# The order of three groups of small products inside a step of attention on TensorE

## The chip, the cores and the metric

The kernel runs on one core of a Trainium2 chip. A time is the device time of one execution in microseconds (us), lower is better; a kernel is described by the median of several executions. TensorE appears in the profile under two names: PE for the matrix products and PEld for the loads of their stationary operands. The other engines are DVE (VectorE), ACT (ScalarE), POOL (GpSimd) and SP (SyncE, which here issues the DMAs).

## What is computed

Attention over 8 batches and 8 heads of 576 rows with 64 columns is followed by a mixture layer on all 4608 rows. The attention has two branches whose outputs are added: a pooled one, in which four neighbouring rows of q, k and v are averaged to 144 rows, and a banded one on the full 576 rows, in which a row sees only those less than 4 rows away.

```python
q_d, k_d, v_d = (t.reshape(B, H, Sd, 4, D).mean(axis=3) for t in (q, k, v))
out_up = np.repeat(sm_attn(q_d, k_d, v_d), 4, axis=2)
mask = np.abs(pos[:, None] - pos[None, :]) < 4
scores = np.where(mask, scale * np.matmul(q, k.transpose(0, 1, 3, 2)), -1e9)
out_local = np.matmul(softmax(scores), v)
x = (out_up + out_local) as [4608, 512]
h = x @ w_in;  g = h * np.clip(h + 3, 0, 6) / 6;  return g @ w_out
```

## The kernel before

A unit of attention is a pair of heads of one batch, 32 units in all. The mixture layer runs over parts of 512 rows; for each of 16 slices of the hidden width its first product (L1056, `gemm1`, 12 matmuls into a PSUM bank called h) is followed by Relu (ACT, L1062), the gate (DVE, L1066), a split into two parts, and the second product (L1106, `gemm2`, 12 matmuls into the banks called o). Two banks, h0 and h1, take turns.

A planner (`Plan.emit`) puts all work of all engines in one order with costs and due times of its own before the program is built; every engine runs its instructions in that order. For units 8 to 31 the products of attention are put on TensorE in steps, one `plan_burst` each. A step handles two units at once: it makes the scores of a new unit and, two units later, the products with v of an old one. 24 units with a lag of two give 22 steps that hold both, two at the start with scores only, and two at the end with products with v only. The planner knows a step as one operation with one cost (2.16 us for both, 1.19 us for one), whatever the order inside.

Inside a step the function `burst` calls three functions in turn. Each matmul in them is a 64x64 one, so that four of them share the array, and each is in float32, which the trace shows as two MATMUL and two LDWEIGHTS instructions.

- `scores_d4` (L537), the pooled scores: four matmuls of 144 columns into the banks a0 and a1, and four of 72 columns into spare columns of h0 and h1. It also takes the four PSUM banks for the step.
- `pv_all`: `pv` (L775), 20 matmuls of 56 to 61 columns, then `pv_d4`, four of 144 columns (L682) and four of 72 (L691). All write h0 or h1.
- `scores` (L732), the banded scores: 20 matmuls of 64 columns into a0 and a1.

After a step ACT copies the 72-column scores out of h0 and h1 (`pull`, L128), ACT and DVE combine the pooled output (`mean`, L707, and `mean_too`, L710), DVE adds the two branches (`add`, L780), which frees h0 and h1 for the first product of the mixture layer, and DVE adds the mask to the banded scores (`outside`, L748) and takes maxima (`top`, L576).

Waits between engines are semaphores. The framework gives a wait to the first instruction that needs it; a wait that the engine has already made earlier in its order is left out. A load of a stationary operand carries a wait itself; further ones stand in instructions of their own ahead of it, EVENT_SEMAPHORE, which the trace puts on TensorE's sequencer (PEldq).

Of the kernel before, what the change touches and what calls it, by code (L numbers as in the profile page):

```python
# [56 lines left out]
def tile_local_down_attention_moe(ctx, tc, q_all, k_all, v_all, _qk_loc, _v_loc, w_in, w_out, ident_d, _mask_d, out):  # L57
# [29 lines left out]
    def view(t, n, shape):  # L87
        t = t[:shape[0], :n]
        names = "abc"[:len(shape) - 1]
        return t if len(shape) == 2 else t.rearrange(  # L90
            f"p ({' '.join(names)}) -> p {' '.join(names)}", **dict(zip(names, shape[1:])))

    def buf(key, holder, shape):

        n = 1
        for k in shape[1:]:
            n *= k
        slot = plan.slot[key, holder]
        if key in late:
            return view(late[key](slot), n, shape)  # L100
        if type(slot[0]) is str:
            tag, first = PLACES[slot[0]]
            if tag not in early:
                early[tag] = wts.tile([P, 2048 if PAIRED[0] <= int(tag[1:]) < PAIRED[1] else 1024], F32, name="early", tag=tag)
            return view(early[tag][:, first + slot[1] // 4:], n, shape)
        at = slot[0]
        if at < XB:
            place = key if key == "rawd" else "xb"
            if place not in early:
                early[place] = mem.tile([P, XB // 4], F32, name="first", tag="first")  # L110
            return view(early[place][:, at // 4:], n, shape)
        if RA[0] <= at < RA[1]:
            return view(taken[:, (at - RA[0]) // 4:], n, shape)
        if at < ARENA:
            t, at = arena, at - XB - (RA[1] - RA[0] if at >= RA[1] else 0)
        else:
            t, at = rounded, at - ARENA
        return view(t[:, at // 4:], n, shape)

    def bank(key, holder):  # L120
        tag = plan.slot[key, holder]
        return psum.tile([P, 512], F32, name=tag, tag=tag)
# [194 lines left out]
    def plan_duo(b, d, masked):  # L317

        bp, b2 = divmod(b, NB2)
        row0 = (bp * P + (b2 * NHP + 2 * d) * NC) * RP  # L320
        k0 = "0" if b == 0 else ""
        PS, kv = ("s", "0") if b == 0 else ("a", "")
        due = need(b) - (1 - d) * 2 * unit_time(b)

        def early_user(o):
            if b == 0:
                early_users.append(o)
            return o

        for u in range(2):  # L330
            unit = plan_unit(b, d, u, row0, k0, kv, PS, masked, early_user, due - (1 - u) * unit_time(b) + SHIFT[NHP * b + 2 * d + u])
            if NHP * b + 2 * d + u < APART:
                for _ in unit:
                    pass
            else:
                plan_burst(unit)

    def plan_burst(unit):

        new = next(unit) if unit else None  # L340
        old = next(units[0]) if len(units) == DEPTH or units and not unit else None
        (b, u), (pb, pu) = (x and x["un"] or (None, None) for x in (new, old))
        key = (b, u) if unit else (pb, pu, "last")
        hx = [(f"h{g}x", key) for g in range(2)]

        def burst():
            hb = [bank(*h) for h in hx]
            if new:
                new["pooled"](hb)
            if old:  # L350
                old["pv"](hb)
            if new:
                new["banded"]()

        both = [x for x in (new, old) if x]
        cost = 2.16 if len(both) == 2 else 1.19
        o = op("PE", cost, burst, [a for x in both for a in x["after"]], take=hx + [t for x in both for t in x["take"]],
               free=[t for x in both for t in x["free"]], lag=LAGT, rec=52 * len(both))
        if old:
            units.pop(0).send((o, hx))  # L360
        if unit:
            unit.send((o, hx))
            units.append(unit)

    def plan_unit(b, d, u, row0, k0, kv, PS, masked, early_user, due):
# [4 lines left out]
        s_ops, sd_ops, turned, pooled = [], [], {}, {}  # L370
# [36 lines left out]
        if b < BY_PE:  # L407
            rk, evs = ("rawd", (0, d)), {}
            for i in (1, 0, 2):
# [3 lines left out]
                                  take=[key, ("qkd" + k0, un)], free=[rk], lag=LAGT, rec=1 if i == 2 else 4))  # L413
# [81 lines left out]
        if direct:  # L495
            sums = [begun["vr"], op({"POOL": on("sum4", 1.0)["POOL"]}, 0, partial(sum4, 0), [begun["v", d]],
                                    take=[("vd" + k0, un)], free=[("raw4", (0, d))])]
# [22 lines left out]
                    nc.tensor.matmul(  # L520
                        ps[hs, j * SD:(j + 1) * SD], q4[hs, j * QSTEP:j * QSTEP + QS], k4[hs], start=True, stop=True)

        def scores_d4(hb):

            for g in range(2):
                st["ps", g] = bank(PS, ("s", un, g))
            st["hb"] = hb
            stats = buf("st" + k0, ("d", un), [P, 2, 12])
            st["md"], st["sd"] = stats[:, 0, :3], stats[:, 1, :3]
            q4, k4 = qk["q", 4], qk["k", 4]  # L530
            for h, j in ((0, 0), (1, 1), (0, 2), (1, 0), (0, 1), (1, 2)):
                hs = slice(h * D, (h + 1) * D)
                a, n = QPLACE[h][j]
                for i in range(2 if n == 2 else 1):
                    ks = slice(i * SD // 2, (i + 1) * SD // 2) if n == 2 else slice(0, SD)
                    ps = rest(h, i) if n == 2 else rows_d4(n)[a * D:(a + 1) * D]
                    nc.tensor.matmul(  # L537
                        ps, q4[hs, j * QSTEP:j * QSTEP + QS], k4[hs, ks], start=True, stop=True, skip_group_check=True)

        def rest(h, i):  # L540
            return st["hb"][h][i * D:(i + 1) * D, HALF + SD:HALF + SD + SD // 2]
# [4 lines left out]
        def rows_d4(n):  # L546
            return st["pd"][:, 2] if n == 2 else st["ps", n][:, 5 * D:5 * D + SD]
# [264 lines left out]
        bk, pk, sk = (PS, ("sd", un)), ("P0" if b == 0 else "Pd", ("d", un)), ("st" + k0, ("d", un))  # L812
        bks = [(PS, ("s", un, g)) for g in range(2)]
        pl, sl = ("P0" if b == 0 else "Pl", ("l", un)), ("st" + k0, ("l", un))
        if apart:
            sd = early_user(op("PE", 0.9, scores_d, [pooled["q"], pooled["k"]], take=[bk, pk, sk], lag=LAGT, rec=12))
        else:
            sd, hx = yield {
                "un": un, "after": turned["q"] + turned["k"] + [pooled["q"], pooled["k"]] + masked,
                "take": [sk] + bks, "free": [], "pooled": scores_d4, "banded": scores}  # L820
            sl_op = sd
        sd_ops.append(sd)
        if apart:
# [14 lines left out]
        if apart:  # L838
            subs = []
            for g in range(2):  # L840
                a = op("DVE", 0.4, lambda g=g: top(rows(g), greatest(g)), [sl_op])
                subs.append(op("DVE", 0.4, lambda g=g: minus(nc.vector, st["p"][:, :, g], rows(g), greatest(g)), [a],
                               free=[bks[g]]))
# [54 lines left out]
        bks = [(PS, ("x", un, g)) for g in range(2)]  # L898
# [6 lines left out]
        else:  # L905
            a, bks = yield {
                "un": un, "after": t + lv + turned_d + sums, "take": [ok] + xbs,
                "free": [tk, vk, tk_d, ("vd" + k0, un)], "pv": pv_all}
# [853 lines left out]
class Plan:  # L1762
# [5 lines left out]
    def op(self, eng, cost, fn, after=(), take=(), free=(), size=0, dl=None, lag=0.0, lock=False, rec=0, nd=1, kind=None):  # L1768
        o = Op(len(self.ops), eng, cost, fn, take, size, dl)
        o.kind = kind  # L1770

        o.rec, o.nd = rec, nd
        o.lag, o.lock = lag, {True: ("DVE", "POOL"), False: ("POOL",)}[lock]
        self.ops.append(o)
        for a in after:
            self.dep(o, a)
        for r in free:
            self.free_after(r, [o])
        return o
# [313 lines left out]
```

## Time and profile before

| | |
|---|---|
| median of 3 executions | 896.09 us (895.85 to 897.17) |
| the profiled execution | 896.23 us, of which the span of instructions is 894.4 us |
| PE busy | 886.5 us, 99% of the span |
| DVE, ACT, POOL busy | 614.4, 430.9, 204.5 us |
| granted TensorE clock | 0.999 |

The profiled execution lies within the runs. Its span is 1.8 us shorter than its time; what lies around the span is the start and end of the launch. The page gives busy times by engine and line; the timeline gives the start of each run of like instructions; the view of a source line lists that line's instructions with the start of the first and the last.

### The profile page before, as it was taken

The page shows a single profiled execution, that of the slowest core. Times are in us where ns is not written, and L with a number is a line of the kernel's source. Part 1 is how long each engine was busy: PE and PEld are TensorE (multiplying, and loading weights), DVE is VectorE, ACT ScalarE, POOL GpSimd, SP SyncE. Part 2 cuts the span into 40 slices and gives each one's busy share as a digit, 9 for nine tenths or more (in the row PEclk, how much of TensorE's full clock was granted, in tenths as well). Part 3 has the DMA queues.
Part 4 walks back from the last instruction along what each step waited for, and adds up shares of the span by engine and source line. Part 5 has one row for each costly group of instructions (what it writes and reads, how often), then busy time and mean ns, then how long its engine had stood idle before and what let it go on. Part 6 is the DMA issues. An engine that isn't in the chain of part 4 may idle for free.

```text
span 894.4 us, 19668 instructions
## 1 busy us (share of the span) xinstructions
PE 886.5 (99%) x7068; PEld 720.9 (81%) x7068; DVE 614.4 (69%) x1164; ACT 430.9 (48%) x1442; POOL 204.5 (23%) x280
## 2 busy tenths in 40 slices
PE   9999999999999999999999999999999999999997
PEld 6677777888888888888888888888888888888886
DVE  7997876666864677657855784667566689876541
ACT  5867754644662456444642563445444155434200
POOL 5624444211512030313221130224112000000000
PEclk9999999999999999999999999999999999999999
DMA  9987543645664456724653667555642221121421
GB/s 234 300 197 250 163 130 89 126 101 102 127 151 95 87 117 140 140 56 102 138 119 77 120 128 202 119 104 114 142 105 59 55 71 48 60 82 70 149 88 48
DMA packets 316178, 107.47 MB, mean 120 GB/s; under 512 B 249520, under 2 KB 295600, under 8 KB 316080
## 3 DMA queue, kind: packets, MB, share of 16 engines
q1 hardware_dynamic: 315478, 105.44, 49.7%
q8 instruction: 56, 0.92, 0.4%
q10 hardware_dynamic: 602, 0.77, 0.3%
q14 instruction: 42, 0.34, 0.1%
HBM read 77.25 MB, written 28.90 MB: 119 GB/s over the span
## 4 chain that ended last, share of the span: by engine, by line
PE 96%; DVE 2%; ACT 1%; POOL 0%; issue 0%; DMA 0%; ACTq 0%; POOLq 0%; DVEq 0%
PE o L1106 35%; PE h L1056 34%; PE o L1321 5%; PE a L1257 5%; PE h L1257 4%; PE h L1321 2%; PE a L1321 2%; PE a L732 2%; PE h L775 2%; PE a L537 1%; PE h L682 1%; PE h L1490 1%; PE a L520 1%; PE a L703 0%; PE h L691 0%; PE h L537 0%
## 5 line engine op out<-in xcount | busy, mean ns | idle before, releaser
L1106 PE MATMUL o<-wp,rounded 128*128 128x512 f32 x1344 | 323.1, 393 | 0.0
L1056 PE MATMUL h<-rounded,wp 128*128 128x512 f32 x1332 | 313.0, 391 | 0.6 <-POOL wp L220 0.5
L1056 PEld LDWEIGHTS h<-rounded,wp 128*128 128x128 f32 x1332 | 248.8, 188 | 54.1 <-issue 1.2
L1106 PEld LDWEIGHTS o<-wp,rounded 128*128 128x128 f32 x1344 | 249.3, 188 | 53.4 <-issue 0.4
L1062 ACT ACTIVATE arena<-h 128x512 f32<-128x512 f32 x111 | 65.8, 593 | 138.6 <-PE h L1056 136.6
L1066 DVE SCALAR_TENSOR_TENSOR arena<-arena,h 128x512 f32<-128x512 f32 x111 | 75.3, 679 | 77.1 <-ACT arena L1062 76.4
L1074 DVE TENSOR_TENSOR rounded<-arena,rounded 128x512 fp32r<-128x512 f32 x75 | 52.7, 703 | 60.4 <-PE o L1106 55.0
L128 ACT CAST rounded<-arena 128x512 fp32r<-128x512 f32 (+5 forms) x87 | 53.6, 618 | 66.9 <-PE o L1106 42.9
L1074 POOL TENSOR_TENSOR rounded<-arena,rounded 128x512 fp32r<-128x512 f32 x37 | 49.3, 1333 | 144.8 <-PE o L1106 124.5
L587 ACT ACTIVATE taken<-taken,arena 128x64 f32<-128x64 f32 x240 | 80.1, 336 | 0.5
L1321 PE MATMUL o<-wp,rounded 128*128 128x512 f32 x192 | 47.8, 392 | 0.0
L130 DVE CAST rounded<-arena 128x512 fp32r<-128x512 f32 (+2 forms) x71 | 30.5, 430 | 22.5 <-PE a L1321 19.5
L587 ACT ACTIVATION_READ_ACCUMULATOR taken<-taken,arena 128x1 f32 x240 | 45.3, 189 | 0.0
L388 DVE STREAM_TRANSPOSE taken<-taken 128x576 f32<-128x576 f32 x56 | 42.7, 767 | 1.3 <-DMA taken<-in_k_dram 0.7
L466 POOL TENSOR_TENSOR arena<-arena 96x256 f32<-96x256 f32 (+1 forms) x21 | 15.4, 733 | 123.3 <-DMA arena<-in_v_dram 123.3
L1321 PEld LDWEIGHTS o<-wp,rounded 128*128 128x128 f32 x192 | 36.0, 188 | 8.0
L464 DVE TENSOR_REDUCE arena<-arena 128x128 f32<-128x512 f32 (+1 forms) x31 | 33.1, 1067 | 13.1 <-PE h L682 10.4
L604 POOL TENSOR_TENSOR taken<-taken,arena 128x432 f32<-128x432 f32 (+1 forms) x21 | 22.6, 1076 | 40.9 <-DVE arena L597 29.4
L563 ACT ACTIVATE arena<-arena 128x1 f32<-128x1 f32 (+1 forms) x78 | 15.1, 193 | 34.5 <-DVE arena L576 34.1
L467 POOL TENSOR_TENSOR arena<-arena 96x128 f32<-96x128 f32 (+1 forms) x21 | 9.5, 453 | 96.9 <-PE h L691 96.4
L128 ACT COPY taken<-h 64x72 f32<-64x72 f32 x96 | 20.3, 211 | 20.2 <-PE h L691 12.3
L420 DVE TENSOR_REDUCE arena<-taken 128x144 f32<-128x576 f32 x38 | 27.9, 747 | 1.9 <-PE h L537 0.8
(260 smaller groups left out, 1213.3 us busy)
## 6 DMA issues: line engine op xcount, KB each, us to landing
taken<-in_v_dram SPq DMA_DIRECT2D x58, 160.0 KB
rawp<-in_w_in_dram SPq DMA_DIRECT2D x16, 512.0 KB
rawp<-in_w_out_dram SPq DMA_DIRECT2D x16, 512.0 KB
taken<-in_q_dram SPq DMA_DIRECT2D x112, 72.0 KB
taken<-in_k_dram SPq DMA_DIRECT2D x112, 72.0 KB
pl<-taken SPq DMA_DIRECT2D x24, 320.0 KB
arena<-pl SPq DMA_DIRECT2D x96, 80.0 KB
arena<-in_v_dram SPq DMA_DIRECT2D x28, 256.0 KB
```

Of the source, the lines that this page charges most:

```text
L128: nc.scalar.copy(out_, in_)
L130: eng.tensor_copy(out_, in_)
L388: nc.vector.transpose(out=qk[kind], in_=qk[kind])
L464: eng.tensor_reduce(out=vd, in_=raw.rearrange("p r e -> p e r"), op=ALU.add, axis=AX.X)
L587: nc.scalar.activation(x[:, j], x[:, j], AF.Exp, bias=m[:, j:j + 1], scale=0.125, accum_out=s[:, j:j + 1])
L1056: nc.tensor.matmul(st["ps"], win[w][:, wt, kk * P:(kk + 1) * P], xs[part][:, kk], start=(kk == 0 and i == 0), stop=(kk == NK - 1 and i == ...
L1062: nc.scalar.activation(st["t"], st["ps"], AF.Relu, bias=3.0)
L1066: nc.vector.scalar_tensor_tensor(out=t, in0=t, scalar=6.0, in1=st["ps"], op0=ALU.min, op1=ALU.mult)
L1074: eng.tensor_tensor(st["gl"], st["t"], st["gh"].bitcast(F32), op=ALU.subtract)
L1106: nc.tensor.matmul(otile[n, m], gt[:, ms], wout[w][:, wt], start=(f == 0 and i == 0), stop=(f == NF - 1 and i == 2),)
L1257: nc.tensor.matmul(ps, w[:, wt, kk * P:(kk + 1) * P], x[part][:, kk], start=start and kk == 0 and i == 0, stop=stop and kk == 1 and i == 2 ...
L1321: nc.tensor.matmul(otile[n + two, m], g[:, m * P:(m + 1) * P], wout[f][:, wt], start=(f == 0 and i == 0), stop=(f == NF - 1 and i == 2), s ...
```

## The change

The order inside a step becomes: banded scores, products with v, pooled scores; and inside the pooled scores the matmuls of 72 columns come ahead of those of 144. Taking the four banks is moved out of `scores_d4` into a function `begin_scores` that runs first. A step without a new unit is as before. What the planner sees is the same: costs, dependencies and buffers of each step.

```diff
         def burst():
             hb = [bank(*h) for h in hx]
             if new:
-                new["pooled"](hb)
+                new["begin"](hb)
+                new["banded"]()
             if old:
                 old["pv"](hb)
             if new:
-                new["banded"]()
+                new["pooled"]()
...
-        def scores_d4(hb):
-
+        def begin_scores(hb):
             for g in range(2):
                 st["ps", g] = bank(PS, ("s", un, g))
             st["hb"] = hb
+
+        def scores_d4():
             stats = buf("st" + k0, ("d", un), [P, 2, 12])
...
-            for h, j in ((0, 0), (1, 1), (0, 2), (1, 0), (0, 1), (1, 2)):
+            for h, j in ((0, 1), (1, 2), (0, 0), (1, 1), (0, 2), (1, 0)):
...
-                "take": [sk] + bks, "free": [], "pooled": scores_d4, "banded": scores}
+                "take": [sk] + bks, "free": [], "begin": begin_scores, "pooled": scores_d4, "banded": scores}
```

## Rows read from the trace of the kernel before

**Rows 1.** Page: busy time of each engine; then the chain's shares by engine.
```profile
PE 886.5 (99%) x7068; PEld 720.9 (81%) x7068; DVE 614.4 (69%) x1164; ACT 430.9 (48%) x1442; POOL 204.5 (23%) x280
...
PE 96%; DVE 2%; ACT 1%; POOL 0%; issue 0%; DMA 0%; ACTq 0%; POOLq 0%; DVEq 0%
```

**Rows 2.** Windows, PE only: stretch, length, busy (instructions), clock, DMA share, GB/s.
```profile
144.00:680.00 536.00, 536.00 (x4707) 1.00 0.55 116
```

**Rows 3.** Timeline of PE, step at 220.61: start, length, line, tiles, shapes, count.
```profile
220.61 0.47 PE L537 MATMUL a<-arena 64*64 64x144 f32 x8
220.90 0.30 PE L537 MATMUL h<-arena 64*64 64x72 f32 x8
221.03 0.76 PE L775 MATMUL h<-arena,taken 64*64 64x60 f32 x40
221.60 0.43 PE L682 MATMUL h<-taken,arena 64*64 64x144 f32 x8
221.86 0.31 PE L691 MATMUL h<-taken,arena 64*64 64x72 f32 x8
221.98 0.76 PE L732 MATMUL a<-taken 64*64 64x64 f32 x40
222.67 0.50 PE L1106 MATMUL o<-wp,rounded 128*128 128x512 f32 x1
```

**Rows 4.** Lines L775, L682, L691 (172:680), L732 (span): durations ns, first, last start.
```profile
L775 PEldq EVENT_SEMAPHORE  x44: 51/51/51, 172.5 to 678.0; - x44
L682 PEldq EVENT_SEMAPHORE  x18: 51/51/51, 173.3 to 678.7; - x18
L691 PEldq EVENT_SEMAPHORE  x34: 51/51/51, 197.5 to 679.1; - x34
L732 PEldq EVENT_SEMAPHORE  x15: 51/51/51, 52.4 to 159.9; - x15
```

**Rows 5.** Timeline of PE, the step at 691.19, which has products with v only.
```profile
691.19 0.81 PE L775 MATMUL h<-arena,taken 64*64 64x60 f32 x40
691.82 0.43 PE L682 MATMUL h<-taken,arena 64*64 64x144 f32 x8
```

**Rows 6.** Timeline of PEld, the same step.
```profile
691.19 0.67 PEld L775 LDWEIGHTS h<-arena,taken 64*64 64x64 f32 x40 [0.35 <-DVE arena L597]
...
691.95 0.28 PEld L691 LDWEIGHTS h<-taken,arena 64*64 64x64 f32 x8
```

**Rows 7.** Source views: L775 in window 686.5:692.4; L691 in window 691.60:691.69.
```profile
L775 PEldq EVENT_SEMAPHORE  x4: 51/51/446, 687.0 to 688.1; - x4
...
L691 PEldq EVENT_SEMAPHORE  x1: 51/51/51, 691.7 to 691.7; - x1
```

**Rows 8.** Timeline of PE, the step at 677.87, the longest of its kind.
```profile
677.87 0.48 PE L537 MATMUL a<-arena 64*64 64x144 f32 x8
...
680.05 0.50 PE L1106 MATMUL o<-wp,rounded 128*128 128x512 f32 x1
```

**Rows 9.** Timeline of PEld, the same step, from its first load on.
```profile
677.87 0.21 PEld L537 LDWEIGHTS a<-arena 64*64 64x64 f32 x8 [0.35 <-issue]
...
679.04 0.29 PEld L691 LDWEIGHTS h<-taken,arena 64*64 64x64 f32 x6
```

**Rows 10.** Source view of L691, windows 677.80:678.97, then 679.07:679.09.
```profile
L691 PEldq EVENT_SEMAPHORE  x1: 51/51/51, 679.0 to 679.0; - x1
...
L691 PEldq EVENT_SEMAPHORE  x1: 51/51/51, 679.1 to 679.1; - x1
```

**Rows 11.** Timeline of PEld, the step at 220.61.
```profile
220.97 0.68 PEld L775 LDWEIGHTS h<-arena,taken 64*64 64x64 f32 x40
...
221.74 0.28 PEld L691 LDWEIGHTS h<-taken,arena 64*64 64x64 f32 x8
```

**Rows 12.** Timelines of ACT, DVE and PE after the step at 220.61.
```profile
222.19 0.29 ACT L707 ACTIVATE arena<-h 128x144 f32<-128x144 f32 x1 [1.09 <-PE h L691]
...
224.19 0.81 DVE L780 TENSOR_TENSOR first<-h,arena 128x288 f32<-128x288 f32 x2
...
225.53 3.33 PE L1056 MATMUL h<-rounded,wp 128*128 128x512 f32 x14
```

## Prediction

> **What bounds the kernel now.** I read the page first: PE is busy 99% of the span and makes up 96% of the chain that ended last [rows 1]. Then the windows: from 144 to 680 us, the stretch that holds all 22 steps with both units, PE is busy for all of its 536.00 us at full clock [rows 2]. So nothing else can end late there, and no wait of PE on another engine costs anything. A change in this stretch can do two things only: lengthen or shorten what PE itself does in a step, or bring a wait on another engine that isn't there now. With no idle time to win, the most that can be gained lies inside the steps.
>
> Then the timeline of one step. It takes 2.06 us from its first product at 220.61 to the next large one at 222.67 [rows 3]. The numbers to read are the distances between groups, not the lengths, since a group's length includes its last product's latency. L775 takes 221.60 - 221.03 = 0.57 us for 40 products, that is ten sets of four, 0.057 us a set. L732 takes 0.69 us with the leaving of the step, L682 0.26 us for two sets of 144 columns, L691 0.12 us for two of 72 [rows 3]. Last I read the sequencer's instructions, EVENT_SEMAPHORE, by line: this is where the order matters.
>
> **The arrangement itself costs nothing.** The same 112 products run in both orders. What could differ is the entry and the exit. Entry: the step that begins with L775 takes 691.82 - 691.19 = 0.63 us for these 40 products [rows 5] against 0.57 in the middle of a step, 0.06 more; the 144-column group takes 220.90 - 220.61 = 0.29 us at the start of a step against 0.26 for L682 in the middle [rows 3], 0.03 more. Both idle times before the first load are 0.35 us [rows 6, 9]. Exit: ten sets of L732 would be 0.57 to 0.58 in the middle of a step and take 0.69 at its end, 0.11 more; I take the same after 144 columns. Sum of the new order: 0.63 + 0.57 + 0.26 + 0.12 + 0.12 + 0.24 + 0.11 = 2.05 us against 2.06. I call it zero, with 0.03 us a step (0.7 us in all) either way.
>
> **Where the waits go.** In a step with both units L775 has two EVENT_SEMAPHOREs (44 in 22 steps), L732 none (the last one of its 15 is at 159.9, before the first of these steps) [rows 4]. In a step with products with v only, L775 has four [rows 7]. The code says why: the first product with v that writes h0, and the first that writes h1, must wait until DVE has read that bank's last contents. In a full step the pooled scores write h0 and h1 first and make these waits; in the other kind L775 makes them itself, one more per bank, and since it also waits for its v and its probabilities, each becomes one more EVENT_SEMAPHORE. In the new order the pooled scores come last, so the products with v are first on h0 and h1 in every step: I expect four EVENT_SEMAPHOREs for L775 instead of two, in two pairs, one pair ahead of the first product and one pair two products later. The banded scores, now first, get waits for their own q and k, which L775's waits covered before.
>
> **What the waits cost.** Such an instruction costs nothing as long as the sequencer is far enough ahead. How far it is ahead depends on what stands before it. Ahead of a step stand large products: the four of the step at 691.19 ran 3 to 4 us early, one of them waited 446 ns, and the idle time before the step was still 0.35 us [rows 6, 7]. So the new waits of the banded scores are free. Inside a step it is much less: the first event of L691 in that step ran at 691.68 to 691.69, while its load began at 691.95 [rows 6, 7], and at that time about two sets of L775 (to 691.82) and the two of L682 were still to start [rows 5]: three and a half to four sets. Four sets of 144 and 60 columns are 0.26 us; four sets of 64 columns, which is what will stand before L775 in the new order, are only about 0.2 us.
>
> The price of a chain of events: in the step at 677.87 two successive ones of L691 begin at 678.97 and 679.08, 0.12 us apart although each is shown with 51 ns, and the load behind the first begins at 679.04, 0.07 us after it [rows 9, 10]. So four in two pairs take 3 x 0.12 + 0.07 = 0.43 us until the load behind the last can begin, and the first pair alone 0.12 + 0.07 = 0.19. The cover is 0.20 us: the first pair fits, the load behind the second pair is 0.43 - 0.21 = 0.22 us late. Not all of it counts: at 677.87 the load behind the second event could begin at 679.08 + 0.07 = 679.15; in a regular step the loads of L691 begin 221.74 - 220.61 = 1.13 us after the start [rows 3, 11], so that this one would be due about 679.01; 0.14 late, and the step is 680.05 - 677.87 = 2.18 us [rows 8], 0.12 longer than 2.06. That also shows that a lag isn't made up: the two places of the array that fell behind kept the step longer by nearly all of it, over the ten sets of L732 that followed. So 0.22 - 0.03 = about 0.19; I take 0.18 us a step, for the first events may run a little earlier than I count. 22 steps: 22 x 0.18 = 4.0 us.
>
> Bounds: with 0.26 us of cover, as in the step at 691.19, the load is 0.16 late and the step 0.13 longer: 2.9 us. With three sets instead of four (0.17 us) it is 0.25 late and 0.22 to 0.25 longer: 5.5 us. Below nothing this term can't go, because a wait that is made later in TensorE's order saves no time where PE never waits [rows 2]. In the two steps with scores only, L732's events move to the start of the step, where they are free, and the pooled scores get none: zero.
>
> The Trainium skill, Perfetto Trace Analysis, Sequencer-only Instruction, says that the profile shows only the execution of such an instruction and neither its decode nor its wait; the trace agrees, with 0.12 us from one to the next where 51 ns are shown.
>
> **What moves for the other engines.** The products with v end about 0.2 us later by their place and 0.2 more by the delay, and the 72-column scores are last in h0 and h1, so L707 and the copies begin some 0.5 us later than now. After the step at 220.61 L707 begins at 222.19, the adds that free h0 and h1 end at 225.00, and the next product into h begins at 225.53 [rows 12], 0.53 us later, which itself moves by 0.2: hidden, and if that cover were gone it would cost the difference. The banks of the banded scores are now last written by the pooled scores, at the same time of the step as now, so L748 and L576 don't move. SP's load of the next v waits for L775 and begins 0.2 to 0.4 us later, the q and k loads up to 1.1 us earlier; both are a whole step ahead of their use. Zero.
>
> Sum: 0 + 4.0 + 0. The profiled execution has 896.23 us, 0.14 more than the median; 896.09 + 4.0 = 900.1 us.
>
> **Rivals.** (1) No cost: the sequencer is further ahead than I read, so that all four events are hidden. For it: one event of 446 ns cost nothing ahead of a step [rows 7], and most events of L691 now cost nothing; against it: the step at 677.87, where events a tenth of a microsecond late lengthened the step [rows 8 to 10]. It decides from a cover of 0.40 us, twice what I read. Time 896.1 (895.6 to 896.8). 13%.
>
> The Trainium skill, TensorE: Matmul & The Clock Gate, gives TensorE's queue 64 places; with four sets' loads and products being 32, that would be eight sets of run-ahead, 0.46 us, and rival 1. The trace reads against it, with about four sets at 691.69.
>
> (2) Part of the cost: the banded scores' waits at the start make one of the two bank waits unnecessary, three events remain, and the load is late by 0.10: 0.07 a step, 1.5 us, 897.6. 9%. (3) More cost: the sequencer, once caught up with, doesn't get ahead again within a step, and the 18 + 34 events of L682 and L691 [rows 4], hidden now, cost up to 0.12 us each, 6.2 us more: 902 to 906. For it: their cover is already thin, as 677.87 shows; against it: there L732 ran at its usual pace afterwards. 9%. (4) Faster: the excess of the few long steps (0.12 at 677.87) vanishes and no cost appears; at most 0.5 us, 895.6, since PE has no idle time to give back. Together with anything not seen, 4%. My forecast: 65%.
>
> **How the numbers follow.** This kernel's measurement tells a difference of about 0.2%, 1.8 us, from none. Slower than 897.9: the forecast, rival 3 and a little of rival 2, 0.75. Same: rival 1, most of rival 2 and the small gains of rival 4, 0.22. Faster by over 1.8 us: 0.03. The range 897.0 to 903.5 holds the forecast with its bounds (899.0 to 901.6), rival 2 and a part of rival 3; rival 1 and the far end of rival 3 are left out, 2 in 10.
>
> **What would show it.** In the profile after: L775 with four EVENT_SEMAPHOREs a step (88 in 22) would show the first step right; two or three, rivals 1 or 2. The full steps 2.2 to 2.3 us long, with gaps between L732 and L775 and two of the four places lagging, would show the second; 2.06 with four events, rival 1. PE still busy without a break and no new wait of L1056 would show the third; a wait of L1056 for L780 would make it wrong. A longer distance between L691's loads and products too would point to rival 3.

## The result and the profile after

The changed kernel takes 902.11 us (median of 4 executions, 900.74 to 902.53) beside 896.63 us for the kernel before (4 executions, 895.85 to 897.97): a ratio of 1.0055, with an interval of 1.0043 to 1.0068. It is 5.5 us slower. The profiled execution is its fastest one, 900.74 us with a span of 898.9, against a span of 894.4 before. Lines below the edit moved by two: L775, L732, L682, L691, L537 are now L777, L734, L684, L693, L539.

The page's busy times and the chain's shares by engine answer to rows 1:

```profile
PE 891.4 (99%) x7068; PEld 722.3 (80%) x7068; DVE 613.5 (68%) x1164; ACT 431.0 (48%) x1442; POOL 205.0 (23%) x280
...
PE 97%; DVE 2%; ACT 1%; POOL 0%; issue 0%; POOLq 0%; DVEq 0%; ACTq 0%
```

PE is busy for 4.9 us longer with the same 7068 instructions, and the other engines do what they did. The profile shows no more idle time on PE: each product counts as busy for about 0.2 us (215 to 262 ns in L777), so products that start a little further apart leave no gap. The windows view of all engines for the stretch of rows 2 (behind the length, the first entry is PE) says the same, 535.94 of 536.00 us busy, with a granted clock of 1.00:

```profile
144.00:680.00 536.00, 535.94 (x4583) 441.42 (x4584) 352.60 (x686) 260.75 (x1062) 129.13 (x192) 1.00 0.55 116
```

The timeline of PE for the step that answers to rows 3:

```profile
221.01 0.81 PE L734 MATMUL a<-taken 64*64 64x64 f32 x40
221.64 0.94 PE L777 MATMUL h<-arena,taken 64*64 64x60 f32 x38
222.37 0.30 PE L684 MATMUL h<-taken,arena 64*64 64x144 f32 x2
222.38 0.25 PE L777 MATMUL h<-arena,taken 64*64 64x61 f32 x2
222.44 0.45 PE L684 MATMUL h<-taken,arena 64*64 64x144 f32 x6
222.62 0.33 PE L693 MATMUL h<-taken,arena 64*64 64x72 f32 x6
...
223.31 0.50 PE L1108 MATMUL o<-wp,rounded 128*128 128x512 f32 x1
```

The step is 223.31 - 221.01 = 2.30 us long; in rows 3 it was 2.06. The difference arises between the first of L777 and L684. From there to the first of L684 there were 0.57 us before (L775 to L682), and there are 0.73 now. Taken in the order of their starts and counted from the first product with v, four of L684's eight records come 0.14 to 0.15 us later than L682's did in rows 3, and four come 0.21 to 0.24 later. The groups also overlap now, the first two of L684 starting before the last two of L777: some of the array's four places (its quarters of 64x64) are behind the others. Behind this point the distances between the groups are the old ones.

Summed over the 22 steps with both units, measured from a step's first product to the next large one, the steps take 50.57 us; before they took 45.61. That is +4.96 us, 0.226 a step, with a median step of 2.302 against 2.065. It explains the 4.5 us that the span grew: the two steps with scores only add 0.07, the first step starts 0.10 earlier, and the stretches behind the steps and at the end of the kernel give back about 0.4. The last us up to the medians' 5.5 is spread among executions, the profiled one being the lowest of its four.

The sequencer's instructions of L777, L684, L693 and L734 in the stretch 172.4 to 690 us answer to rows 4 (count, durations in ns, first and last start):

```profile
L777 PEldq EVENT_SEMAPHORE  x85: 51/51/51, 172.9 to 683.5; - x85
...
L684 PEldq EVENT_SEMAPHORE  x18: 51/51/51, 173.6 to 684.0; - x18
...
L693 PEldq EVENT_SEMAPHORE  x34: 51/51/51, 198.0 to 684.2; - x34
...
L734 PEldq EVENT_SEMAPHORE  x91: 51/51/51, 192.5 to 679.1; - x91
```

L777 has 85 where L775 had 44 [rows 4]; L684 and L693 have the 18 and 34 that L682 and L691 had. L734 has new ones, which run some 4 us ahead of their step. Where the events of L777 lie in the step at 221.01 is read from narrow windows of the source view, 221.38 to 221.41, 221.49 to 221.52, 221.61 to 221.64 and 221.72 to 221.75:

```profile
L777 PEldq EVENT_SEMAPHORE  x1: 51/51/51, 221.4 to 221.4; - x1
...
L777 PEldq EVENT_SEMAPHORE  x1: 51/51/51, 221.5 to 221.5; - x1
...
L777 PEldq EVENT_SEMAPHORE  x1: 51/51/51, 221.6 to 221.6; - x1
...
L777 PEldq EVENT_SEMAPHORE  x1: 51/51/51, 221.7 to 221.7; - x1
```

In the trace they begin at 0.381, 0.492, 0.618 and 0.724 us after the step's start. The load behind the last one is found in the same way, in PEld's timeline with windows from 221.750 to 221.806 and then to 221.812; it is the third load of the second window:

```profile
221.65 0.16 PEld L777 LDWEIGHTS h<-arena,taken 64*64 64x64 f32 x2
...
221.65 0.29 PEld L777 LDWEIGHTS h<-arena,taken 64*64 64x64 f32 x3
```

So it begins at 221.81, that is 0.80 us after the start and 0.076 after the last event. Without a delay it would have begun at about 0.58, with the load of the first product: 0.22 late. The chain sets its own pace: 15 of the 19 steps with four events have them at these four offsets to within 0.003 us, which waits for other engines or for transfers would not give, and in the three steps with three events, too, the load comes 0.076 us behind the last one.

### The profile page after: what moved, and what is told of

It reads as the page before. It is cut to its first block, busy times and chain, and to the rows that moved or that the text cites. A ratio compares the mean times of both kernels' runs of the same rounds, so it can differ in the third digit from the quotient of the medians.

```text
span 898.9 us, 19751 instructions
## 1 busy us (share of the span) xinstructions
PE 891.4 (99%) x7068; PEld 722.3 (80%) x7068; DVE 613.5 (68%) x1164; ACT 431.0 (48%) x1442; POOL 205.0 (23%) x280
## 4 chain that ended last, share of the span: by engine, by line
PE 97%; DVE 2%; ACT 1%; POOL 0%; issue 0%; POOLq 0%; DVEq 0%; ACTq 0%
PE o L1108 35%; PE h L1058 33%; PE o L1323 5%; PE a L1259 5%; PE h L1259 4%; PE a L1323 2%; PE h L1323 2%; PE a L734 2%; PE h L777 2%; PE a L539 1%; PE h L684 1%; PE h L1492 1%; PE a L521 0%; PE a L705 0%; PE h L693 0%; PE a L777 0%
```

## The experiments

The theory: the step is longer because four waits stand in front of the products with v, in a chain of about 0.42 us that has only the run-ahead behind the banded scores, about 0.2 us, to hide in. (The cover of a chain is the time that the instructions queued ahead of it still take.) Rivals: the new order of the groups costs by itself, whatever the waits do; an event costs time wherever it stands; the inner order of the pooled scores (the second half of the change) matters. Each kernel below is the changed kernel with another `burst` or another list of products; the work is the same in all.

**The same waits, far ahead.** The products with v run first, behind large products:

```diff
             if new:
                 new["begin"](hb)
-                new["banded"]()
             if old:
                 old["pv"](hb)
             if new:
+                new["banded"]()
                 new["pooled"]()
```

> Order of a step: products with v, banded scores, pooled scores. L777 keeps its four event instructions, but they now stand behind large products, 3 to 4 us ahead. My theory: they are free there, as in the two steps with products with v only; full steps 2.05 to 2.08, time 896.4 (895.8 to 897.2), as the kernel before. Rival, four events cost what they cost wherever they stand: 901 to 902.5. Rival, pooled scores at the end of a step delay what frees the banks: above 898, with a wait of L1058 in the profile.

Measured: 897.58 us, 1.0006 times the kernel before (0.9997 to 1.0015). The timeline of PE for one step, and the events of L777 over all steps:

```profile
222.12 0.81 PE L777 MATMUL h<-arena,taken 64*64 64x60 f32 x40
...
223.12 0.76 PE L734 MATMUL a<-taken 64*64 64x64 f32 x40
...
224.19 0.50 PE L1108 MATMUL o<-wp,rounded 128*128 128x512 f32 x1
...
L777 PEldq EVENT_SEMAPHORE  x86: 51/51/51, 172.6 to 689.8; - x86
```

As many events as in the changed kernel, and steps of 2.07 us. The events of the step at 222.12 ran from 218.0 to 219.0. So an event costs nothing where the sequencer is far ahead, and what counts is its place. That rules out the rival by which an event costs wherever it stands. The step is as expected; the time lies above the expected interval, and the kernel before, run alongside, has 897.34 us, 1.25 more than the median that the prediction started from.

**Pooled scores ahead of the products with v.** They make the bank waits again, and lie between the banded scores and L776 (this kernel's line of the products with v):

```diff
                 new["banded"]()
+                new["pooled"]()
             if old:
                 old["pv"](hb)
-            if new:
-                new["pooled"]()
```

> Order of a step: banded scores, 72-column scores, 144-column scores, products with v. The banded scores are still first, but the 72-column scores make the bank waits, and two sets of 144 columns stand directly ahead of the products with v. My theory: two event instructions for L777, hidden, full steps 2.05 to 2.08, time 896.8 (896 to 897.6), as the kernel before. Rival, the banded scores at the start of the step cost by themselves: above 899.

Measured: 898.48 us, 1.0016 (1.0007 to 1.0025).

```profile
221.93 0.81 PE L733 MATMUL a<-taken 64*64 64x64 f32 x40
...
222.93 0.76 PE L776 MATMUL h<-arena,taken 64*64 64x60 f32 x40
...
224.00 0.50 PE L1107 MATMUL o<-wp,rounded 128*128 128x512 f32 x1
...
L776 PEldq EVENT_SEMAPHORE  x47: 51/51/51, 174.4 to 690.0; - x47
```

The steps are as expected: two events, 2.07 us, and 0.15 us more than before in the sum of all 22. The banded scores are first here and the pooled scores are last in the kernel above; neither entry nor exit costs anything, so inside the steps the order by itself doesn't. The time is 1.6 us above that of the kernel before all the same, clear of noise and outside the expected interval, and the steps don't hold it. In the profile the first step begins at 145.19 us instead of 143.98, although the program up to it is the same (over the profiles of all kernels it begins between 143.9 and 145.4), and 17 of the 25 stretches between steps are longer by 0.04 us and one by 0.22, some 0.86 in all, of which the few shorter stretches and above all the end of the kernel give back 0.75. The kernel above has the same 0.04, the latest first step of all, and a time only 0.2 us above before. What causes this was not found.

**Only the 72-column scores ahead.** They alone write h0 and h1, so they alone have to be early:

```diff
             if new:
                 new["begin"](hb)
+                new["pooled"](((0, 1), (1, 2)))
                 new["banded"]()
...
-                new["pooled"]()
+                new["pooled"](((0, 0), (1, 1), (0, 2), (1, 0)))
...
-        def scores_d4():
+        def scores_d4(some=((0, 1), (1, 2), (0, 0), (1, 1), (0, 2), (1, 0))):
...
-            for h, j in ((0, 1), (1, 2), (0, 0), (1, 1), (0, 2), (1, 0)):
+            for h, j in some:
```

> Order of a step: the four 72-column pooled scores, banded scores, products with v, 144-column pooled scores. The 72-column scores write h0 and h1 first, at the start of the step, and make the two bank waits there; L777 keeps two event instructions as in the kernel before, still with only four sets of 64 columns ahead of them. My theory (the chain of four events that the bank waits make ahead of the products with v costs about 0.23 us in each of 22 steps): full steps of 2.06 to 2.08 us, time 896.6 (896 to 897.5). Rival, the place of the groups itself costs (banded ahead of products with v, 144 columns at the end): steps stay at 2.30, time 901 to 902.5.

Measured: 897.38 us, 1.0003 (0.9994 to 1.0012). PE's timeline and the events of the products with v (here L778) in one step:

```profile
220.95 0.36 PE L540 MATMUL h<-arena 64*64 64x72 f32 x8
221.13 0.76 PE L735 MATMUL a<-taken 64*64 64x64 f32 x40
221.71 0.78 PE L778 MATMUL h<-arena,taken 64*64 64x60 f32 x40
...
223.04 0.73 PE L1109 MATMUL o<-wp,rounded 128*128 128x512 f32 x2
...
L778 PEldq EVENT_SEMAPHORE  x2: 51/51/51, 221.5 to 221.6; - x2
```

Eight records moved to the front take the 5.5 us away: two events are left, and L778 to the next group takes 0.577 us (0.575 before). The median step is 2.089, 0.024 above before. In the trace L778's third load comes 0.08 us behind the second event and the fourth 0.03 behind that, as the first two held loads of the changed kernel do (0.800 and 0.835); so the two events seem to lie at the edge of their cover, which was not tested.

**Only the 144-column scores ahead of the products with v.** They write a0 and a1 and take no bank wait away, but they stand in front of L778 and lengthen its cover. The edit is the one above with the other four pairs, placed behind `banded`:

```diff
                 new["banded"]()
+                new["pooled"](((0, 0), (1, 1), (0, 2), (1, 0)))
             if old:
                 old["pv"](hb)
             if new:
-                new["pooled"]()
+                new["pooled"](((0, 1), (1, 2)))
```

> Order of a step: banded scores, the four 144-column pooled scores, products with v, the four 72-column ones. Four event instructions ahead of the products with v as in the changed kernel, but two of the four sets that hide them are now of 144 columns and take 0.12 us instead of 0.06. My theory (what counts is the time of the work queued ahead of the chain): about 0.12 us of the 0.24 remain, full steps 2.17 to 2.20, time 899 (898 to 900). Rival, four events cost the same wherever they stand inside a step: steps 2.30, time 901 to 902.5. Rival, the place of the 72-column scores behind the products with v delays the copies and so PE: time as in the changed kernel, with a wait of L1058 for ACT or DVE in the profile.

Measured: 900.01 us, 1.0029 (1.0018 to 1.0039), a median step of 2.174.

```profile
222.21 0.81 PE L735 MATMUL a<-taken 64*64 64x64 f32 x40
222.84 0.43 PE L540 MATMUL a<-arena 64*64 64x144 f32 x8
223.09 0.81 PE L778 MATMUL h<-arena,taken 64*64 64x60 f32 x38
...
224.38 0.49 PE L1109 MATMUL o<-wp,rounded 128*128 128x512 f32 x1
...
L778 PEldq EVENT_SEMAPHORE  x4: 51/51/51, 222.7 to 223.1; - x4
```

The four events are back, and the step costs 0.11 us instead of 0.24: as many waits behind longer products cost half. This is the sharpest test of the theory. In both kernels the first event runs when 28 loads and products ahead of it are still to start; here these take 0.13 us longer, so that it comes 0.38 us before the first product with v instead of 0.25, and the load behind the last event still follows it after 0.077. The steps with three events are hidden or nearly so, 2.068 to 2.097 us. The 144-column products have left the end of the step as well, but the two kernels with covered waits show that such a move costs nothing there.

**The inner order.** Inside the pooled scores the products of 144 columns go first again, all else as in the changed kernel:

```diff
-            for h, j in ((0, 1), (1, 2), (0, 0), (1, 1), (0, 2), (1, 0)):
+            for h, j in ((0, 0), (1, 1), (0, 2), (1, 0), (0, 1), (1, 2)):
```

> The changed kernel with the second half of the change undone: inside the pooled scores the 144-column products come first and the 72-column ones last, both still behind the products with v. Four event instructions and four sets of 64 columns ahead of them, as in the changed kernel. My theory: full steps 2.29 to 2.31, time 902 (901 to 902.8), as the changed kernel. Rival, the inner order matters for PE, because the copies out of h0 and h1 begin 0.25 us later: a wait of L1058 for ACT or DVE and 903 or more; or it matters for the array: below 901.

Measured: 901.77 us, 1.0052 (1.0039 to 1.0064), a median step of 2.303 with the events of L777 still 85. The second half of the change is worth nothing in this place.

**One bank's wait early: a miss.** Of the 72-column scores only those of h0 go first:

```diff
                 new["begin"](hb)
+                new["pooled"](((0, 1),))
                 new["banded"]()
...
-                new["pooled"]()
+                new["pooled"](((1, 2), (0, 0), (1, 1), (0, 2), (1, 0)))
```

> Half the dose: of the 72-column scores only those in h0 come at the start of the step, so only the wait for h1 is left to the products with v; order: two 72-column products, banded scores, products with v, the rest of the pooled scores. L777 should have three event instructions a step instead of four (two in the kernel before). My theory: the load behind the last is about 0.11 us late, full steps 2.17 to 2.20, time 899 (898.3 to 900). Rival, only the number of changes of order matters and not the events: 901 to 902.5; rival, one bank wait alone is hidden: 896.6.

Measured: 902.55 us, 1.0060 (1.0047 to 1.0072): one event fewer than the changed kernel, and no faster. **And the same with h1's**, `((1, 2),)` first and `((0, 1), ...)` in the rest:

> As the half dose with h0 first, with the two banks exchanged: the two 72-column products of h1 at the start of the step, those of h0 at the end. Again three event instructions for L777 instead of four. With h0 first the step came out at 2.32 us instead of the 2.17 to 2.20 that I expected. Explanation to be tried: the events hold up the products on partitions 64 to 127 (they need the bank h1 or the later loads), and with h0 first this half of the array also has its 72-column work at the end, so that both lags add; 0.06 us of it shows in steps with scores only (1.17 against 1.11). With h1 first the late half has done its extra work and the other half has its own at the end, so that the lags lie beside each other: full steps 2.11 to 2.20, time 898 to 899.5. Rival, three events ahead of the products cost what they cost with h0 first, whichever half waits: 2.30 to 2.34, 901.5 to 903.

Measured: 898.29 us, 1.0014 (1.0005 to 1.0022). The time is in the expected interval, but not for the expected reason. The events of L778 over all steps, of the kernel with h0 first and then of the one with h1 first:

```profile
L778 PEldq EVENT_SEMAPHORE  x65: 51/51/51, 173.1 to 684.6; - x65
```

```profile
L778 PEldq EVENT_SEMAPHORE  x46: 51/51/51, 173.8 to 689.3; - x46
```

Three in 19 of 22 steps in the one and two in every step of the other (the last two of its 46 belong to the next step, with products with v only). DVE frees h1 after h0 and both are waits for a value of the same semaphore, so that having waited for h1 covers h0, but not the reverse: in the trace the load behind the third event waits for DVE with h0 first, and no load of L778 does with h1 first. So this pair doesn't compare like with like. But each shows where its time goes.

By the code the 72-column products of one head run on two of the four places only, and they hold these for 0.12 us at the start of the step (two records after each other). The trace of the kernel with h0 first has the three events 0.507, 0.632 and 0.742 us after the start of the step at 237.45, where the changed kernel has its four from 0.381 to 0.724: they come in TensorE's order, and the work of the two loaded places is ahead of them. The first four loads of L778 are for just these two places, which are 0.12 us behind anyway, and begin at 0.70. The fifth is the first one for the other two, behind the third event. In PEld's timeline it is the load by which these two windows differ, 238.160 to 238.262 and to 238.272, so that it begins at 238.27, 0.82 after the start:

```profile
238.15 0.20 PEld L778 LDWEIGHTS h<-arena,taken 64*64 64x64 f32 x4
...
238.15 0.25 PEld L778 LDWEIGHTS h<-arena,taken 64*64 64x64 f32 x5
```

In the changed kernel these two places get their first load of this group at 0.80. They have the same work behind it here, since h1's 72 columns still stand at the end. So they are as late with three events as with four, and the step is as long: 2.320 against 2.302. One event fewer does shorten the chain, as in the three-event steps of the changed kernel (load at 0.69); in this kernel, too, the two steps with two events take only 2.21 and 2.24 us. The step of the expectation that failed is the start of the chain: it began 0.12 later, behind two products that held up only half of the array.

With h1 first the loaded places are the other two. The first loads of L778 go to the free ones, at 0.59 with one event ahead, and the fourth load, for a loaded place, follows at 0.70, when that place is free: hardly anything is late. What is left is 2.120 - 2.065 = 0.055 us for the uneven load, as in the steps with scores only of both kernels, 1.17 against 1.114. The times are read from the trace; which place a load is for follows from the code and the order of the records, since the trace doesn't name it. A kernel with a free order of the heads in the products with v, which would test it, was not run.

The median full step and the sum over the 22 steps, with the time against the kernel before, run alongside each:

| kernel | order in a step | events of pv | step | sum less before's | time less before's |
|---|---|---|---|---|---|
| before | pooled, pv, banded | 2 | 2.065 | 0 | 0 |
| changed | banded, pv, pooled | 4 | 2.302 | 4.96 | 5.5 |
| inner order undone | banded, pv, pooled | 4 | 2.303 | 5.16 | 4.9 |
| 144 ahead of pv | banded, 144, pv, 72 | 4 | 2.174 | 2.17 | 2.7 |
| 72 first | 72, banded, pv, 144 | 2 | 2.089 | 0.42 | 0.0 |
| pooled ahead of pv | banded, pooled, pv | 2 | 2.068 | 0.15 | 1.6 |
| pv first | pv, banded, pooled | 4, far ahead | 2.068 | 0.09 | 0.2 |
| h0's 72 first | 72 of h0, banded, pv, rest | 3 | 2.320 | 5.45 | 5.2 |
| h1's 72 first | 72 of h1, banded, pv, rest | 2 | 2.120 | 1.08 | 1.4 |

None is faster than the kernel before: PE has no idle time in this stretch, and the order before already keeps the waits covered in nearly all of its steps (2.064 to 2.18 us, the median 2.065).

## Why the prediction was right, and where it was not

**The arrangement costs nothing: right.** Taken as zero with 0.03 us a step either way; the two kernels with other orders and covered waits have steps of 2.068 against 2.065. That is shown for the steps; the 1.6 us of one of these kernels outside its steps has no known cause.

**Four events instead of two: right.** 85 in 22 steps and not 88: three steps have three. The records of the trace name the semaphores. L777's events wait for DMAs alone, those that bring v (two, by the code) and the probabilities (four), one or two in each event, and the wait for DVE, the bank's, stands on the load behind each bank's events. In L775 that load carried one of the DMA waits. So the bank's wait takes the load's place, and the wait that it displaces needs one event more per bank, as predicted. The three steps with three events are those in which only five DMA waits are left instead of six. They are a dose in between, inside the changed kernel itself. PE's timeline and L777's events of one of them:

```profile
296.68 0.81 PE L734 MATMUL a<-taken 64*64 64x64 f32 x40
...
298.87 0.50 PE L1108 MATMUL o<-wp,rounded 128*128 128x512 f32 x1
...
L777 PEldq EVENT_SEMAPHORE  x3: 51/51/51, 297.1 to 297.3; - x3
```

2.195 us, between the 2.065 without uncovered events and the 2.302 with the full chain. The third event costs 0.13 and the fourth 0.11 us.

**Chain and cover: right.** Predicted were 0.43 us from the first event to the load behind the last, and a load 0.22 late; measured are 0.80 - 0.38 = 0.42 and 0.22. The first pair was predicted to fit, and does: L777 starts 0.63 us after the step's start, and ten sets at a step's start take 0.63 us where nothing is late [rows 5].

**What of it counts: wrong in size.** "So 0.22 - 0.03 = about 0.19; I take 0.18 us a step". The deduction came from the one lag that the trace of before showed, 0.14 late for a step that was 0.12 longer. Here 0.22 late makes a step 0.237 longer, and in the three-event step the load begins at 0.694, some 0.11 late, for a step 0.13 longer. The step grew by what its most belated place had lost at L684, 0.24 us, and nothing was made up. At 677.87 before, too, the last two products of L691 start 1.41 and 1.45 us after the step's start; in the step of rows 3 they start at 1.33. That is 0.09 and 0.12 late, and the step was 0.12 longer:

```profile
679.28 0.22 PE L691 MATMUL h<-taken,arena 64*64 64x72 f32 x1
...
679.31 0.22 PE L691 MATMUL h<-taken,arena 64*64 64x72 f32 x1
```

So the 0.03 us that were taken off came from measuring the lag at a load: a regular load of L691 begins 0.12 us before its product [rows 3, 11] and can be late by a part of that for nothing. With 0.226 us as the mean of the 22 steps, the one mis-sized term is 4.96 us instead of 4.0. That is half of the 2.0 us between the 900.1 predicted and the 902.11 measured. Of the rest, 0.54 is the median of before, 896.63 in these executions and 896.09 in those that the prediction started from, and about 0.5 isn't accounted for, less than the spread of the changed kernel's own executions (1.8). The term's upper bound, 5.5 us, held it.

**The banded scores' new waits are free: right.** 91 events, and the idle time ahead of a step is 0.35 us as before. One of the two steps with scores only is 1.184 instead of 1.112; the other one has the same order and takes 1.114, so the order isn't its cause.

**Consumers: right.** ACT, DVE and PE behind the step at 221.01, which answer to rows 12:

```profile
223.11 0.29 ACT L709 ACTIVATE arena<-h 128x144 f32<-128x144 f32 x1 [1.60 <-PE h L539]
...
225.10 0.81 DVE L782 TENSOR_TENSOR first<-h,arena 128x288 f32<-128x288 f32 x2
...
226.21 1.98 PE L1058 MATMUL h<-rounded,wp 128*128 128x512 f32 x8
```

L709 begins 2.10 us after the step's start and now waits for the pooled scores (L539); before, it began 1.58 after. The adds end at 225.10 + 0.81 = 225.91, and the next product into h begins at 226.21, 0.30 us later. The margin fell from 0.53 to 0.30 us and was not used up; PE has no new wait.

**The rivals.** No cost at all, which needs a run-ahead of twice four sets, is ruled out by the events' places: the first ran 0.2 us ahead of its load, with about three and a half sets of loads and products still to start, some 28 instructions. A queue of 64 places, which the Trainium skill gives (TensorE: Matmul & The Clock Gate, Architectural detail), would by estimate have hidden the chain; the trace doesn't agree, with these 28. Part of the cost, by which the banded scores' waits make a bank's wait unnecessary, didn't come: the load behind each bank's events waits for DVE in all 22 steps, also in the three with three events. More cost, by which the events of L684 and L693 would show up too, didn't come: their number is unchanged, and the distances behind L684 are those of before. As rival 4 says, the excess of the step at 677.87 [rows 8] is gone (the same step takes 2.302 now, as the others do), but the cost came. A few steps are longer than the rest, the worst one 2.45 us:

```profile
563.76 0.81 PE L734 MATMUL a<-taken 64*64 64x64 f32 x40
...
566.21 0.50 PE L1108 MATMUL o<-wp,rounded 128*128 128x512 f32 x1
...
L777 PEldq EVENT_SEMAPHORE  x4: 51/51/51, 564.1 to 564.6; - x4
```

Its third event begins 0.15 us later than in a regular step. It is not a wait that was not yet met: the event waits for one DMA semaphore, and in the trace the last transfer that counted on it had landed 6.1 us before the step began. What held it is open; it is 0.15 us once.

## What to carry to other kernels

When a group of short products is moved, ask which instruction will now be the first to touch each buffer: that one inherits the waits that the old first one made for all, and in this kernel these waits cost time where the work queued ahead of them was short. Put the group with the most waits at the start of a burst, behind long products, or let a few cheap products that touch the same buffers go first: here eight records moved to the front were worth 5.5 us. Where several waits go to one semaphore, making the latest first saves the others, as the kernel with h1's products first shows.

## What was unexpected in the hardware

- An EVENT_SEMAPHORE of TensorE is shown with 51 ns, but in this chain one follows another after 0.11 to 0.125 us, and the load behind the last comes after 0.076. The hidden part is more than half of the price.
- A place of the array that has fallen behind doesn't catch up: a load 0.22 us late makes the step 0.237 longer, although some 17 sets of four records still follow in it.
- Products on different places need not start in program order: L684 starts at 222.37, L777's last two at 222.38.
- Stretches of large products behind a step are longer by 0.04 us in several of the kernels, without a difference in what runs there. The cause is open.
